# Range-check counts loaded ahead of the last chunk, its products in another order, and u's transposes in four PSUM buffers copied by two engines

## The chip, the cores and the metric

The kernel runs on one core of one Trainium2 chip. A core has a matrix engine (TensorE; PE in the profile, with its weight loads as PEld), a vector engine (VectorE, DVE), a scalar engine (ScalarE, ACT), GpSimd (POOL) and a queue engine that issues DMAs (SyncE, SP). Matmuls write to PSUM, a small memory in banks, and VectorE or ScalarE carry the results from there to SBUF, the working memory. Each engine works through its own list of instructions in the order in which they were written, and waits on semaphores for the others.

The metric is the device time of one execution in microseconds (us). The profile's span, from the first to the last instruction, is some 2 us shorter than that time.

## The reference

Two blocks follow each other. The first is attention with routing: for each of 4 batches and 8 heads, 768 queries and keys of 64 numbers are assigned to one of 16 centroids, and a query sees only the keys of its own centroid. The second is an MLP mixer over the 768 tokens of 512 channels:

```
scores = where(q_assign == k_assign, q @ k.T / 8, -1e9)
x      = softmax(scores) @ v            # heads side by side: (4, 768, 512)
h      = relu(x.T @ w_tok1) @ w_tok2    # over tokens, 768 -> 256 -> 768
u      = x + h.T
out    = u + relu(u @ w_ch1) @ w_ch2    # over channels, 512 -> 1536 -> 512
```

All of it is float32. The change lies in the last line of this, the channel products, and in what follows them.

## The kernel before

The work runs in three stages. Up to about 326 us, 16 pairs of heads go through the attention. Up to about 414 us come the token products: `tok1` and `tok2` of all four batches, which leave u in `xs[b]`, a tile of 128 partitions x 6 row blocks x 512 channels for each batch. The rest is the channel products of the four batches.

**The channel products.** Each is a product of 2 x 2 blocks, done with seven block products where the plain way has eight (a scheme of Strassen's kind): `left_weights`, `right_weights` and `turn_u` prepare sums and differences of the blocks, and `chunk` runs the seven products of one piece. A batch has two parts, and each part has three chunks of the first product (`ch1_chunk`, w_ch1 and the relu, results `h2`) and three chunks of the second (`ch2_chunk`, w_ch2, results added to `xs[b]` and, in part 1, sent to the output). A block product of `ch2_chunk` is three matmuls over 128 x 128 x 256, each of which the trace shows as two, so "x6" is one product.

**A chunk.** The products go to three PSUM tiles, tags X, Y and Z, of which pool `ps_m` has two buffers each. The order is written out by hand: p1 in X, then the left-over product c21 of the chunk before (list `late`, in that chunk's X), p5 in Z, c11 in Y, u2 in X, c12 in Z, c22 in X. Every product is followed by its `done`, which reads the PSUM tile: in `ch2_chunk` always a VectorE add, for p1, p5 and u2 into a kept tile, for the others into u. X is used again and again: u2, c22 and c21 go on adding to what p1 left in it, each after the result before it has been read. Z takes c12 on top of p5 in the same way. In part 1, c12 completes one block of 128 rows of the output and c21 another, and SyncE then issues its DMA (L707). After the very last chunk, `late.pop()()` runs its c21, so that c22 and c21 stand side by side there.

**turn_u.** Before the channel products of a batch, u must be transposed: `turn_u(b, n)` makes, for one half n of the rows, four PSUM tiles `pt` (f = 0 to 3) of three TensorE transposes each, and copies each to `uT`. With n = 1 it ends with four subtractions on VectorE, which make the sums `uTs` and change `uT`. It is called eight times: twice for batch 0 among the last `tok2` products, and for each later batch after the first and the second `ch2_chunk` of part 1 of the batch before. All four tiles have the tag Y, and ScalarE copies all four. The `tok2` products around the first two calls use the tags X and Z in turn (`mtile`).

**The range check.** The fast way is right only if certain sums lie in a range. `fits` and `fits_count` count the good partitions, early (about 529 us). `fits_load` reads the three counts into registers of every engine, and at L1077 every engine branches over a slow general version (`general`) if all are good, as they are here. `fits_load` stands behind everything else, after the last chunk. On SyncE each load comes with a check of its bounds.

Of the kernel before, what the change touches and what calls it, by code (L numbers as in the profile page):

```python
# [8 lines left out]
F32 = mybir.dt.float32  # L9
# [7 lines left out]
B, H, S, D = 4, 8, 768, 64  # L17
C = 16
P = 128
NJ = S // P  # L20
DM = H * D
# [5 lines left out]
HJ = NJ // 2  # L27
# [20 lines left out]
def kernel(  # L48
# [29 lines left out]
    nc = tc.nc  # L78
# [30 lines left out]
    pools = {}  # L109
# [424 lines left out]
    def sub(dst, a, b):  # L534
        nc.vector.tensor_tensor(out=dst, in0=a, in1=b, op=ALU.subtract)

    def add(dst, a, b):
        nc.vector.tensor_tensor(out=dst, in0=a, in1=b, op=ALU.add)  # L538
# [36 lines left out]
    def turn_u(b, n):  # L575

        if n == 0:
            pools["uT"] = pools["u"].tile([P, 2, NF, HS], F32, name="uT")
            pools["uTs"] = pools["u"].tile([P, 3, NF // 2, HS], F32, name="uTs")
        uT, uTs = pools["uT"], pools["uTs"]  # L580
        for f in range(NF):
            pt = pools["ps_m"].tile([P, HJ, P], F32, tag="Y", name="pt")
            for i in range(HJ):
                nc.tensor.transpose(  # L584
                    out=pt[:, i], in_=xs[b][:, HJ * n + i, f * P : (f + 1) * P], identity=ident
                )
            nc.scalar.copy(out=uT[:, n, f], in_=pt.rearrange("p i t -> p (i t)"))
        if n == 1:
            R = {"B11": uT[:, 0, 0:2], "B21": uT[:, 0, 2:4], "B22": uT[:, 1, 2:4]}
            R["T1"], R["T2"], R["T4"] = (uTs[:, i] for i in range(3))  # L590
            R["T3"] = b12 = uT[:, 1, 0:2]
            sub(R["T1"], b12, R["B11"])
            sub(R["T2"], R["B22"], R["T1"])
            sub(R["T3"], R["B22"], b12)
            sub(R["T4"], R["B21"], R["T2"])
            pools["R"] = R

    late = []

    def chunk(n, product, done):  # L600


        def ptile(tag):
            return pools["ps_m"].tile([P, n], F32, tag=tag, name="p" + tag)

        X = ptile("X")
        product(X, "A11", "B11", True)
        if late:
            late.pop()()
        done("p1", X)  # L610
        Z = ptile("Z")
        product(Z, "S1", "T1", True)
        done("p5", Z)
        Y = ptile("Y")
        product(Y, "A12", "B21", True)
        done("c11", Y)
        product(X, "S2", "T2", False)
        done("u2", X)
        product(Z, "S4", "B22", False)
        done("c12", Z)  # L620
        product(X, "S3", "T3", False)
        done("c22", X)

        def end():
            product(X, "A22", "T4", False)
            done("c21", X)

        late.append(end)

    def ch1_chunk(part, i):  # L630
# [17 lines left out]
        def done(name, psum):  # L648
# [24 lines left out]
            else:  # L673
                a = h2["A12"][:, i]
                nc.scalar.activation(out=a, in_=psum, func=ACT.Relu)
                sub(h2["S4"][:, i], a, h2["S2"][:, i])

        chunk(HS, product, done)

    def ch2_chunk(b, part, i):  # L680

        h2, Bw = pools["h2"], pools["B"]
        u = {
            f"c{r + 1}{c + 1}": xs[b][:, HJ * r + i, 256 * c : 256 * c + 256]
            for r in range(2)
            for c in range(2)
        }
        kept = {}
        takes = {"p1": "c11", "p5": "c22", "u2": "c12"}
        gives = {"c11": "p1", "c22": "p5", "c12": "u2"}  # L690

        def product(psum, a, w, start):
            for k in range(3):
                nc.tensor.matmul(  # L694
                    psum, lhsT=h2[a][:, k, i * P : (i + 1) * P], rhs=Bw[w][:, 3 * part + k],
                    start=start and k == 0, stop=k == 2, skip_group_check=not start,
                )

        def done(name, psum):
            if name in takes:  # L700
                kept[name] = pools["mlp"].tile([P, DM // 2], F32, name=name, bufs=2)
                add(kept[name], psum, u[takes[name]])
            else:
                add(u[name], psum, kept[gives[name]] if name in gives else u[name])
                if part == 1 and name in ("c12", "c21"):
                    j = i + HJ * (name == "c21")
                    nc.sync.dma_start(  # L707
                        out[b].rearrange("(p j) m -> p j m", p=P)[:, j], xs[b][:, j]
                    )

        chunk(DM // 2, product, done)

    good = const.tile([P, 3], F32, name="good")
    count = const.tile([1, 3], I32, name="count")
# [22 lines left out]
    def fits_load():  # L737

        loaded = [
            nc.values_load(count[0:1, i : i + 1], min_val=0, max_val=P) for i in range(3)  # L740
        ]
        return loaded[0] + loaded[1] + loaded[2]
# [127 lines left out]
    while ends:  # L870
        for _ in range(-(-len(beside) // len(ends))):
            beside.pop(0)()
        ends.pop(0)()
        if len(ends) in (11, 9):
            turn_u(0, len(ends) == 9)
# [4 lines left out]
    for b in range(B):  # L880
        for part in range(2):
            for i in range(3):
                ch1_chunk(part, i)
                for _ in range(2):
                    if beside:
                        beside.pop(0)()
            for i in range(3):
                ch2_chunk(b, part, i)
                if part == 1 and i < 2 and b + 1 < B:
                    turn_u(b + 1, i)  # L890
            if b == 0:
                (fits_count if part else fits)()
    late.pop()()
    both = fits_load()


    def general():
# [209 lines left out]
```

## Time and profile before

| What | Measured |
|---|---|
| time, median of 3 runs | 873.44 us (873.29 to 873.79) |
| span of the profiled execution | 871.6 us |
| granted TensorE clock, mean | 0.997 |
| transposes of turn_u (L584) | 96, median 273 ns a record, first at 394.2, last at 744.1 |
| copies of turn_u (L587) | 32 on ScalarE, median 479 ns |
| one VectorE copy of the same shape (L776) | 558 ns |
| matmul of a ch2 product (L694) | 379 ns a record |
| VectorE add of a ch2 product (L538) | 0.42 us |
| output DMAs (L707) | 24 of 256 KB, median 2.0 us from issue to landing |
| last matmuls start | 862.50 us |
| last add starts | 864.10 us |

How to read it: records of matmuls overlap, since the engine starts the next before the last one's modelled end; the pace of a row is the distance between starts, not the length of a record. In a timeline the columns are the start, the length from the first record's start to the last one's end, the engine, the line, the operation with output and inputs, the count, and in brackets how long the engine was idle before and who released it. In the view of one line of code the columns are engine, operation, count, the shortest, median and longest duration in ns, and the first and last start. A "q" behind an engine's name marks its own queue of control instructions (register loads, branches, semaphore events), which do not count as busy.

### The profile page before, as it was taken

How to read it: one execution, taken by the hardware profiler on the slowest of the kernel's cores; microseconds unless marked ns; L12 is line 12 of the kernel's file. 1: busy time of each engine (PE TensorE's matmuls, PEld its weight loads, DVE VectorE, ACT ScalarE, POOL GpSimd, SP SyncE). 2: the span in 40 equal slices, each digit the busy share in tenths (PEclk: the TensorE clock that was granted, in tenths of full speed). 3: DMA queues.
4: the chain of work that ended last, by engine and by line, in shares of the span. 5: the costliest groups of instructions: out<-in, count | busy, mean ns of one | idle time of the engine just before them, and what ended most of it. 6: DMA issues, size and time to landing. Idle time of an engine off the chain costs nothing.

```text
span 871.6 us, 11036 instructions
## 1 busy us (share of the span) xinstructions
PE 858.7 (99%) x4294; PEld 525.3 (60%) x4294; DVE 502.8 (58%) x848; ACT 296.6 (34%) x506; POOL 45.7 (5%) x40
## 2 busy tenths in 40 slices
PE   9999999999999999999999999999999999999996
PEld 4444444445444444444577686785876867768675
DVE  6878887989888852894553443424344333443332
ACT  5566566666656541421210312103112021130210
POOL 1001010101101000320000000000000000000000
PEclk9999999999999999999999999999999999999998
DMA  7855455576563300510000010000010000100001
GB/s 147 150 122 111 91 119 112 121 104 139 125 116 94 86 25 1 168 49 1 0 1 1 0 37 37 0 1 1 36 37 1 0 1 25 49 1 1 0 26 51
DMA packets 133275, 47.61 MB, mean 55 GB/s; under 512 B 122080, under 2 KB 126176, under 8 KB 133216
## 3 DMA queue, kind: packets, MB, share of 16 engines
q1 hardware_dynamic: 131616, 46.45, 24.0%
q8 instruction: 35, 0.57, 0.3%
q10 hardware_dynamic: 1600, 0.39, 0.2%
q14 instruction: 24, 0.20, 0.1%
HBM read 34.64 MB, written 6.29 MB: 47 GB/s over the span
## 4 chain that ended last, share of the span: by engine, by line
PE 94%; DVE 4%; ACT 1%; issue 0%; DVEq 0%
PE sc L420 18%; PE pX L694 14%; PE pX L643 14%; PE av L443 14%; PE pZ L694 7%; PE pZ L643 7%; PE ph L512 4%; PE pY L694 4%; PE pY L643 4%; PE pu L521 3%; PE px L472 1%; PE small L459 1%; PE pt L584 1%; PE small L301 1%; DVE wh L214 1%; DVE wT L219 1%
## 5 line engine op out<-in xcount | busy, mean ns | idle before, releaser
L425 ACT ACTIVATE ex<-sc 128x768 f32<-128x768 f32 x192 | 151.4, 812 | 71.1 <-PE av L443 36.5
L420 PE MATMUL sc<-qkT 64*128 64x384 f32 x768 | 155.0, 482 | 0.0
L433 DVE TENSOR_TENSOR sum<-sum,ex 128x768 f32<-128x768 f32 x128 | 127.7, 997 | 28.3 <-ACT ex L425 15.6
L443 PE MATMUL av<-ex,va 128*64 128x384 f32 x768 | 127.4, 488 | 0.0
L443 PEld LDWEIGHTS av<-ex,va 128*64 128x64 f32 x768 | 53.7, 137 | 71.7 <-issue 69.9
L420 PEld LDWEIGHTS sc<-qkT 64*128 64x128 f32 x768 | 67.9, 187 | 39.4 <-issue 39.4
L643 PE MATMUL pX<-uT,wc 128*128 128x384 f32 x192 | 67.4, 487 | 0.0
L420 PE MATMUL sc<-ohT 64*128 64x384 bf16 x384 | 62.7, 323 | 0.2 <-DVE ohT L393 0.2
L651 ACT COPY p<-pX 128x384 f32<-128x384 f32 x24 | 11.4, 475 | 148.1 <-PE pX L643 148.1
L643 PEld LDWEIGHTS pX<-uT,wc 128*128 128x128 f32 x192 | 36.2, 190 | 24.7 <-issue 1.0
L226 POOL TENSOR_TENSOR wc<-wT,wup 128x512 int32<-128x512 int32 x24 | 33.1, 1378 | 199.9 <-DVE wT L219 199.9
L512 PE MATMUL ph<-x,wt 128*128 128x512 f32 x96 | 42.1, 594 | 0.7 <-DVE x L524 0.7
L521 PE MATMUL pu<-h,wt 128*128 128x512 f32 x96 | 42.0, 592 | 0.0
L538 DVE TENSOR_TENSOR c<-pZ,u 128x384 f32<-128x384 f32 x24 | 13.4, 558 | 46.8 <-PE pZ L643 46.8
L420 PEld LDWEIGHTS <-ohT 64*128 64x128 bf16 x384 | 18.7, 94 | 33.2 <-issue 9.4
L538 DVE TENSOR_TENSOR x<-pX,x 128x256 f32<-128x256 f32 x24 | 10.2, 424 | 49.3 <-PE pX L694 49.3
L538 DVE TENSOR_TENSOR hA<-pY,p 128x384 f32<-128x384 f32 x24 | 13.4, 557 | 40.4 <-PE pY L643 40.4
L694 PE MATMUL pX<-w2s,hA 128*128 128x256 f32 x144 | 35.1, 380 | 0.5 <-DVE x L538 0.5
L694 PE MATMUL pX<-wc,hA 128*128 128x256 f32 x144 | 35.0, 379 | 0.0
L694 PE MATMUL pZ<-w2s,hS 128*128 128x256 f32 x144 | 35.0, 379 | 0.0
L694 PE MATMUL pY<-wc,hA 128*128 128x256 f32 x144 | 35.0, 379 | 0.0
L694 PE MATMUL pX<-w2s,hS 128*128 128x256 f32 x144 | 35.0, 379 | 0.0
(126 smaller groups left out, 1173.3 us busy)
## 6 DMA issues: line engine op xcount, KB each, us to landing
raw<-in_moe_w_ch_dram SPq DMA_DIRECT2D x24, 512.0 KB, 4.1
va<-in_v_dram SPq DMA_DIRECT2D x16, 384.0 KB, 3.2
out_dram<-x SPq DMA_DIRECT2D x24, 256.0 KB, 2.0
qk<-in_k_dram SPq DMA_DIRECT2D x60, 96.0 KB, 3.8
qk<-in_q_dram SPq DMA_DIRECT2D x60, 96.0 KB, 3.6
raw<-in_moe_w_tok_dram SPq DMA_DIRECT2D x3, 512.0 KB, 4.5
raw<-in_moe_w_tok_dram SPq DMA_DIRECT2D x4, 384.0 KB, 4.0
ex<-in_q_dram ACTq DMA_DIRECT2D x4, 96.0 KB, 3.3
```

The costliest lines, as they stand in the source:

```text
L214: nc.vector.tensor_scalar(out=h, in0=h, scalar1=0x07FFFFFF, scalar2=3, op0=ALU.bitwise_and, op1=ALU.logical_shift_left,)
L226: nc.gpsimd.tensor_tensor(out=dst.bitcast(I32), in0=T, in1=up, op=ALU.add)
L420: nc.tensor.matmul(sc[:, h, 0:HS], lhsT=src[rows, 1, j], rhs=src[rows, 0, js], start=start, stop=not start,)
L425: nc.scalar.activation(out=ex, in_=sc[:, :, 0:HS], func=ACT.Exp, scale=SM_SCALE)
L433: nc.vector.tensor_tensor(out=acc, in0=acc if j > 1 else st["ex", qh, 0], in1=st["ex", qh, j], op=ALU.add)
L443: nc.tensor.matmul(av[h * D : (h + 1) * D], lhsT=st["va"][:, h, j], rhs=ex[:, h], start=(j == 0), stop=(j == NJ - 1),)
L512: nc.tensor.matmul(pf, lhsT=W["tok1"][:, j, t * P : (t + 1) * P], rhs=xs[b][:, j], start=(j == 0), stop=(j == NJ - 1),)
L521: nc.tensor.matmul(pu, lhsT=W["tok2"][:, t, j], rhs=h1s[b][:, t], start=(t == 0), stop=(t == NT - 1))
L538: nc.vector.tensor_tensor(out=dst, in0=a, in1=b, op=ALU.add)
L643: nc.tensor.matmul(psum, lhsT=A[a][:, k, c * P : (c + 1) * P], rhs=R[r][:, k], start=start and k == 0, stop=k == 1, skip_group_check=not s ...
L651: nc.scalar.copy(out=kept[name], in_=psum)
L694: nc.tensor.matmul(psum, lhsT=h2[a][:, k, i * P : (i + 1) * P], rhs=Bw[w][:, 3 * part + k], start=start and k == 0, stop=k == 2, skip_grou ...
```

## The change

Three edits, in two groups.

The first group is in `turn_u`: the tiles pt take the tags Y and Z in turn, so that with two buffers each all four of a call have one of their own; and the copies of f = 1 and f = 3 go to VectorE. It is for letting the transposes of a call run without waiting for their copies.

The second group is at the end. `chunk` gets a flag for the very last chunk, which changes the order of its products from p1, (c21 before), p5, c11, u2, c12, c22, c21 to p1, (c21 before), p5, u2, c11, c22, c12, c21. It is for putting a product of another tile between the two that use X. And `fits_load` moves from behind everything to ahead of that last chunk, so that the engines have the counts in their registers by the end.

```diff
@@ turn_u
-            pt = pools["ps_m"].tile([P, HJ, P], F32, tag="Y", name="pt")
+            pt = pools["ps_m"].tile([P, HJ, P], F32, tag="YZ"[f % 2], name="pt")
...
-            nc.scalar.copy(out=uT[:, n, f], in_=pt.rearrange("p i t -> p (i t)"))
+            copy = nc.vector.tensor_copy if f % 2 else nc.scalar.copy
+            copy(out=uT[:, n, f], in_=pt.rearrange("p i t -> p (i t)"))
@@ chunk
-    def chunk(n, product, done):
+    def chunk(n, product, done, last=False):
...
-        product(Y, "A12", "B21", True)
-        done("c11", Y)
+
+        def product_y():
+            product(Y, "A12", "B21", True)
+            done("c11", Y)
+
+        def product_z():
+            product(Z, "S4", "B22", False)
+            done("c12", Z)
+
+
+        between = [product_y, product_z]
+        if not last:
+            between.pop(0)()
         product(X, "S2", "T2", False)
         done("u2", X)
-        product(Z, "S4", "B22", False)
-        done("c12", Z)
+        between.pop(0)()
         product(X, "S3", "T3", False)
         done("c22", X)
+        if last:
+            between.pop(0)()
@@ ch2_chunk
-        chunk(DM // 2, product, done)
+        chunk(DM // 2, product, done, b == B - 1 and part == 1 and i == 2)
@@ the loop over the batches
             for i in range(3):
+                if b == B - 1 and part == 1 and i == 2:
+                    both = fits_load()
                 ch2_chunk(b, part, i)
...
     late.pop()()
-    both = fits_load()
```

## The prediction

> **What bounds the kernel now.** I read the page first: the share of each engine, then the tenths in 40 slices, then the chain that ended last.
>
> ```profile
> span 871.6 us, 11036 instructions
> ...
> PE 858.7 (99%) x4294; PEld 525.3 (60%) x4294; DVE 502.8 (58%) x848; ACT 296.6 (34%) x506; POOL 45.7 (5%) x40
> ...
> PE 94%; DVE 4%; ACT 1%; issue 0%; DVEq 0%
> ```
>
> TensorE (PE) is busy 99% of the span and is 94% of the chain, at a granted clock of 0.997. VectorE (DVE) stands at 58%, ScalarE (ACT) at 34%, and in the second half, where the change lies, at 3 to 4 and 0 to 2 tenths a slice. So time comes only from three places: holes in the stream of matmuls, extra matmuls (the change has none), and what runs after the last matmul. The list of waits has the holes that concern the change:
>
> ```profile
> PEld pt L584 <- ACT uT L587: 3.8, 8, 0.5
> ...
> PE pt L584 <- ACT uT L587: 1.9, 8, 0.2
> ...
> PE pX L694 <- DVE x L538: 0.5, 1, 0.5
> ```
>
> Columns: total us, times, longest. Eight times, once in each call of turn_u, the transposes wait for ScalarE's copies; once, at the end, a product waits for a VectorE add. Then the timeline of one turn (of the eight, all alike):
>
> ```profile
> 517.59 0.82 PE L584 MATMUL pt<-ident,x 128*128 128x128 f32 x6
> 517.79 0.42 DVE L538 TENSOR_TENSOR x<-pX,p 128x256 f32<-128x256 f32 x1 [0.87 <-PE pX L694]
> 518.12 0.86 ACT L587 COPY uT<-pt 128x384 f32<-128x384 f32 x2 [8.91 <-PE pt L584]
> ...
> 518.65 0.93 PE L584 MATMUL pt<-ident,x 128*128 128x128 f32 x6 [0.24 <-ACT uT L587]
> ...
> 519.41 0.38 PE L694 MATMUL pX<-wc,hA 128*128 128x256 f32 x1
> ```
>
> Six transposes start within 0.82 us; the last one's record is 0.273 us long (the median of that row), so they start (0.82 - 0.273)/5 = 0.109 us apart. Twelve would take 1.31 us. The turn takes 519.41 - 517.59 = 1.82. **The hole is 0.51 us a turn**, more than the 0.24 that the wait shows, since a matmul's modelled end lies behind the start of the next. Last, the tail: the timeline's last add, and the engines' own queues at the lines of the register loads (L740) and of the branch (L1077).
>
> ```profile
> 864.10 0.42 DVE L538 TENSOR_TENSOR x<-pX,x 128x256 f32<-128x256 f32 x1 [1.65 <-PE pX L694]
> ```
> ```profile
> L740 PEldq TENSOR_LOAD <-count x3: 306/306/495, 862.5 to 863.5; - x3
> ...
> L740 SPq TENSOR_LOAD <-count x3: 262/280/519, 864.9 to 866.4; - x3
> ```
> ```profile
> L1077 PEldq COMPARE_BRANCH  x1: 3336/3336/3336, 864.0 to 864.0; - x1
> ...
> L1077 SPq COMPARE_BRANCH  x1: 58/58/58, 867.1 to 867.1; - x1
> ```
>
> The last add ends at 864.52, SyncE (SP) issues the last output until 864.88, and only then loads its three counts, one after the other, each with its bounds check; it reaches the branch at 867.1, its next semaphore event at 869.6, and the span ends at 871.6. SP is the last engine there: PE's next event is at 867.4, DVE's at 868.6.
>
> [...] from branch to next event it is 2.5 us on SP, 2.7 on ACT, 2.9 on DVE, 3.4 on PE, and 0.2 on POOL. This stays in the changed kernel. [...] a DVE copy of 128x384 from 6.80 for 0.56 us overlaps an ACT copy from 7.12 for 0.48, each at its usual length.
>
> **Part A, the transposes.** Each turn makes four tiles of three transposes. Two buffers (tag Y) become four (Y, Z, Y, Z), and the second and fourth copies move to VectorE, so no tile of a turn waits for a copy of the same turn. Gain at most 8 x 0.51 = 4.1 us.
> What takes some of it back:
> - Are the Z buffers free? In the six turns among the channel products, the last Z product is c12, whose add ends about 0.7 us before the turn (in the chunk before it, 516.49 + 0.42 = 516.9 against 517.59): nothing. In the first two turns the last tok2 tile is a Z tile and its add runs beside the transposes (394.80 + 0.69 = 395.49); the fourth tile's weight load would come at 394.60 + 8 x 0.109 = 395.47, and a release takes some 0.05: 0.07 us each, 0.14 in all.
> - A VectorE copy of this shape costs 0.56 us (one row, L776, 558 ns; ACT 479), 32 copies becoming 16 and 16. Behind it in the turns with n = 0 nothing waits for over 3 us (DVE's next add is at 511.31 in the turn at 506.70): nothing. With n = 1 the four subtractions of uTs (0.875 us apart) are queued behind it. Now they start at 519.01. Then: fourth tile ready at 517.59 + 11 x 0.109 + 0.273 = 519.06, copy from 519.10, first subtraction at about 519.57 (a 384-element pass passes the engine in 0.47), the second after the first has ended, 520.65, the fourth at 522.4, then the adds for c21 at 523.27 and p1 at 523.6, which ends at 524.02. The product u2 waits for this p1 add, because it goes on adding to X. It would start at 518.90 + 4 x 1.296 = 524.08, its weights 0.2 earlier, so it is 0.1 us late, 0.2 at most; in three turns 0.3 (0 to 0.6). Before, p1's add had ended at 523.49 against 524.60.
>
> A gains 4.1 - 0.14 - 0.3 = **3.65** (3.3 to 4.1).
>
> **Part B, order of the last chunk.** Now c22 and c21 stand side by side in X, so c21 waits until c22's result is added: its matmul starts at 862.50, where 860.53 + 1.296 = 861.82 was due, and its own pace is disturbed by a further 0.10 (the record is 1.56 us instead of 1.46). With c12, in Z, between them, c22's add (0.42 + 0.2) lies beside c12's 1.296. Gain 0.68 + 0.10 = 0.78. The other neighbours, p5 then u2: u2 needs p1's add, which ends at 856.30, against its start at 856.64: nothing. The row of output that c12 completes goes out 1.3 us later, still 1.3 us ahead of the last one: nothing.
>
> **Part B, the counts.** On SP, 864.88 to 867.1 shrinks to the branch's own arithmetic, some 0.15 us: 2.05 gained. The loads' new place costs SP nothing (idle from 852.5 to 856.0; they need 2.1). DVE passes them behind c22's add at 852.96, done by 854.5, and its next add is due at 855.55. ACT and POOL have none of the chunk's work. On PE they stand behind the c22 product of the chunk before, which is released when u2's add ends, about 850.84; from there c12 and c22 give work until 852.75, and the loads take 1.3 us (862.51 to 863.83 now), ending at 852.2, with the next product's weight load due at 852.54: nothing, if the queue holds those 18 instructions and a load needs no idle engine. It needs none at 862.51, where it starts with 1.2 us of that product still to be issued.
> Against this, SP's fetch now begins at 864.3, while the last output is on its way. Undisturbed it took 2.5; DVE's, at that place, 2.9; PE's 3.4. I take 2.9: 0.4 lost (0 to 0.9).
>
> B gains 0.78 + 2.05 - 0.4 = **2.4** (1.9 to 2.8). PE and DVE, without their loads, pass their branches earlier too and stay ahead of SP.
>
> **Sum**: 873.44 - 3.65 - 2.4 = **867.4**.
>
> **Rivals.**
> 1. VectorE becomes a bound in the turns with n = 1: the copies push the subtractions further than I think and u2 takes back all of 0.51 in three turns, and the fourth tiles wait longer in the first two. A is then 8 x 0.51 - 3 x 0.51 - 0.3 = 2.3: 868.7. For: a margin of nearly zero. Against: my chain already charges the second subtraction a full wait on the first.
> 2. PE's loads drain it: from the end of c22, 852.9, 1.3 us of loads and a cold start, 1.5 lost: 868.9. Against: the start at 862.51.
> 3. The tail is set by something not seen in it (the landing of the last output, or fetches that hinder each other), and B gives its 0.78 alone: 869.0.
> 4. Slower: copies of two engines hinder each other and the transposes, so that each turn loses 0.4 instead of gaining (+3.2), PE's loads drain it (+1.5), and B gains 2.4: +2.3, 875.7. Nothing but the unknown speaks for it.
>
> **Chances.** My sum 0.73 (866.5 to 868.1), rival 1 0.09, rival 2 0.10, rival 3 0.04, rival 4 0.02, a mild failure of both parts that ends near no change 0.02. The range runs from 866.4, all bounds good, to 868.9, which takes in the first two rivals. Faster by 0.2% (below 871.7): 0.96; within 0.02; slower 0.02.
>
> **What the profile after would show.** Turns of 1.31 us from first transpose to next matmul, about 1.38 in the first two; no wait of PE for uT; COPY rows of L587 on ACT x16 and DVE x16. p1's add after the turns with n = 1 ending within 0.2 us of u2's start. No wait of PE for x in the last chunk; its matmuls 1.296 apart to the end. PE's loads at about 850.8 less A's gain, with no hole at the next product; SP's branch within 0.3 us of its last issue. I am wrong if a hole of over 1 us follows PE's loads, if turns stay over 1.5 us, or if SP's wait behind the branch grows past 3.4 us.

## The result, and the profile after

The changed kernel takes **867.35 us** (median of 6 runs, 866.91 to 867.70) against 873.43 (873.29 to 873.79): a ratio of 0.993 with a 95% interval of 0.9917 to 0.9943, 6.1 us or 0.7% faster. A second set of runs gave 866.95 against 873.45, 6.5 us.

First the page of the changed kernel, its head and its chain. The counts of engine instructions show what was moved: 16 copies from ACT (506 to 490) to DVE (848 to 864).

```profile
span 864.8 us, 11041 instructions
...
PE 856.0 (99%) x4294; PEld 525.0 (61%) x4294; DVE 511.0 (59%) x864; ACT 290.7 (34%) x490; POOL 45.8 (5%) x40
...
PE 94%; DVE 4%; issue 0%; DMA 0%; DVEq 0%; ACT 0%
```

PE's work is the same 4294 matmuls, in a span 6.8 us shorter. Next the timeline of the turn that the prediction showed, in the changed kernel, and on to the product u2.

```profile
515.83 1.47 PE L584 MATMUL pt<-ident,x 128*128 128x128 f32 x12
...
516.36 0.48 ACT L588 COPY uT<-pt 128x384 f32<-128x384 f32 x1 [9.24 <-PE pt L584]
516.69 1.21 DVE L588 COPY uT<-pt 128x384 f32<-128x384 f32 x2 [0.23 <-PE pt L584]
517.01 0.48 ACT L588 COPY uT<-pt 128x384 f32<-128x384 f32 x1 [0.17 <-PE pt L584]
...
517.14 1.46 PE L707 MATMUL pX<-wc,hA 128*128 128x256 f32 x6
517.82 0.95 DVE L535 TENSOR_TENSOR uTs<-uT 128x768 f32<-128x768 f32 x1
...
521.82 0.41 DVE L538 TENSOR_TENSOR p<-pX,x 128x256 f32<-128x256 f32 x1
...
522.29 0.73 PEld L707 LDWEIGHTS pX<-w2s,hS 128*128 128x128 f32 x4 [0.20 <-DVE p L538]
```

All twelve transposes now stand in one row without a wait, and the turn takes 517.14 - 515.83 = 1.31 us. The price is in the lower half: VectorE's copies end at 517.90, the first subtraction starts 1.99 us after the turn (1.42 before), p1's add ends at 522.23, and the weight load of u2, due at about 522.11, comes at 522.29. It stands 0.2 us ahead of its matmul, so of these 0.18 us only 0.07 reach the row of matmuls. Then the tail: the last products in the timeline, and the engines' own queues at the line of the loads (now L753) and of the branch (L1091).

```profile
855.10 1.46 PE L707 MATMUL pX<-wc,hS 128*128 128x256 f32 x6
...
856.39 1.46 PE L707 MATMUL pZ<-wc,hS 128*128 128x256 f32 x6
...
857.69 1.46 PE L707 MATMUL pX<-w2s,hA 128*128 128x256 f32 x6
...
858.34 1.63 SPq L720 DMA_DIRECT2D out_dram<-x  x2
859.19 0.42 DVE L538 TENSOR_TENSOR x<-pX,x 128x256 f32<-128x256 f32 x1 [0.87 <-PE pX L707]
```
```profile
L753 PEldq TENSOR_LOAD <-count x3: 305/306/495, 846.7 to 847.7; - x3
L753 SPq TENSOR_LOAD <-count x3: 267/278/514, 848.4 to 849.8; - x3
```
```profile
L1091 SPq EVENT_SEMAPHORE  x8: 17/17/17, 862.9 to 863.5; - x8
...
L1091 SPq COMPARE_BRANCH  x1: 57/57/57, 860.1 to 860.1; - x1
```

c22, c12 and c21 start 1.29 to 1.30 us apart, up to the end. The loads on PE run from 846.73 to 848.04, and the timeline around them goes on at its pace (848.62 - 847.33 = 1.29):

```profile
847.33 1.46 PE L707 MATMUL pX<-wc,hS 128*128 128x256 f32 x6
...
848.41 1.27 PEld L707 LDWEIGHTS pX<-wc,hA 128*128 128x128 f32 x6
848.62 1.46 PE L707 MATMUL pX<-wc,hA 128*128 128x256 f32 x6
```

SP's last issue ends at 859.97 and its branch stands at 860.1, where 2.2 us lay between them before. Its next event comes 2.8 us behind the branch, where it was 2.5. The prediction and the expectations call such a wait a fetch; that it is one was the author's inference and is not shown.

### The profile page after: what moved, and what is told of

Same layout as the page of the kernel before. It is cut to its first block, busy times and chain, and to the rows that moved or that the text cites. A ratio compares the mean times of both kernels' runs of the same rounds, so it can differ in the third digit from the quotient of the medians.

```text
span 864.8 us, 11041 instructions
## 1 busy us (share of the span) xinstructions
PE 856.0 (99%) x4294; PEld 525.0 (61%) x4294; DVE 511.0 (59%) x864; ACT 290.7 (34%) x490; POOL 45.8 (5%) x40
## 4 chain that ended last, share of the span: by engine, by line
PE 94%; DVE 4%; issue 0%; DMA 0%; DVEq 0%; ACT 0%
PE sc L420 18%; PE pX L707 14%; PE pX L656 14%; PE av L443 14%; PE pZ L707 7%; PE pZ L656 7%; PE ph L512 4%; PE pY L707 4%; PE pY L656 4%; PE pu L521 3%; PE px L472 1%; PE small L459 1%; PE pt L584 1%; PE small L301 1%; DVE wh L214 1%; DVE wT L219 1%
```

## The experiments

All are edits of the changed kernel or, for one part alone, of it with the other parts put back. Each time stands against that of the kernel before, measured beside it. "PE's last matmul" below is the end of its record in the trace, less the difference with which the two traces start (see the repeat).

**The changed kernel again**, as a yardstick.

> The changed kernel itself, once more, as the yardstick for the runs beside it. Theory (holes closed, loads hidden): 867.35 us as before, turns of 1.31 us, three holes of 0.07 us before u2 after the turns with n = 1, no hole at TensorE's register loads. The first measurements spread over 866.9 to 867.7 where the kernel before spreads over 873.3 to 873.8; if the spread is in the fetch behind SyncE's branch, this profile shows there another length than 2.73 us; if it is in the loads at the start, another offset of the first matmuls.

Measured: 866.95 us (866.88 to 867.79). The turns, the three small holes and SP's wait behind the branch (from the branch's start to the next event, 2.79 us in both profiles of this kernel; 2.73 from its end) are the same to 0.01 us. What differs is the start: one early group of transposes, in the timelines of this run and of the first one.

```profile
12.41 0.51 PE L385 MATMUL po<-identb,oh 128*128 128x128 bf16 x6
```
```profile
12.12 0.51 PE L385 MATMUL po<-identb,oh 128*128 128x128 bf16 x6
```

In the kernel before it stands at 12.40. So some 0.3 us of the spread between runs is decided in the first 12 us, which the change does not touch; what decides it there stays open.

**Part A alone.**

```diff
-                if b == B - 1 and part == 1 and i == 2:
-                    both = fits_load()
...
-        chunk(DM // 2, product, done, b == B - 1 and part == 1 and i == 2)
+        chunk(DM // 2, product, done)
...
     late.pop()()
+    both = fits_load()
```

> Part A alone: four buffers and two engines in turn_u; order and loads at the end as before. Theory: eight holes of 0.51 us go, three of 0.07 come: 873.43 - 3.9 = 869.5. Rival (the gain is mostly in the tail): above 871.

Measured: 869.86 us against 873.66, ratio 0.9954 (0.9941 to 0.9968): 3.8 us. PE's last matmul ends 3.86 us sooner than in the kernel before, and the hole of 0.68 before it is back.

**The order alone** (turn_u and the loads as before).

> Of part B only the order of the products in the last chunk; turn_u and loads as before. Theory: the hole of 0.68 us before the last product and the 0.10 in it go, everything behind them moves by 0.78: 872.65; SyncE's fetch stays at 2.5 us. Rival (the end is set by the output DMAs or another engine): 873.4.

Measured: 872.97 us against 873.66, ratio 0.9992 (0.9985 to 0.9999): 0.7 us. The timeline of PE in this run has the last four products at an even pace:

```profile
858.39 1.46 PE L707 MATMUL pY<-wc,hA 128*128 128x256 f32 x6
859.69 1.46 PE L707 MATMUL pX<-wc,hS 128*128 128x256 f32 x6
860.98 1.46 PE L707 MATMUL pZ<-wc,hS 128*128 128x256 f32 x6
862.28 1.46 PE L707 MATMUL pX<-w2s,hA 128*128 128x256 f32 x6
```

Behind the branch SP waits 2.6 us, as before within 0.1.

**The early loads alone** (turn_u and the order as before).

> Of part B only the register loads ahead of the last chunk; order and turn_u as before. Theory: SyncE goes from its last issue to the branch 2.05 us sooner, its fetch takes 2.75 us instead of 2.5 since the last output is then on its way: 873.43 - 1.8 = 871.6; no hole in the matmuls at TensorE's loads. Rival (TensorE's loads cost it a pause that other gains covered): 872.9.

Measured: 871.68 us against 873.66, ratio 0.9977 (0.9968 to 0.9987): 2.0 us. PE's matmuls run without a hole past its loads. The branch's line in this run:

```profile
L1091 SPq EVENT_SEMAPHORE  x8: 17/17/17, 868.2 to 868.7; - x8
...
L1091 SPq COMPARE_BRANCH  x1: 58/58/58, 865.4 to 865.4; - x1
```

2.8 us from branch to event, with the last issue ending at 865.26. In the runs where SP branches after its loads (before, part A alone, order alone) it is 2.53 to 2.61; in those where it branches right behind the last issue, 2.70 to 2.90. That the output in flight is what lengthens the wait fits both groups. So does another cause: SP's wait overlaps VectorE's by 1.5 to 2.0 us in the first group and by 2.1 to 2.4 in the second, so the two waits may hinder each other. Nothing here shows either or separates the two.

The three parts sum to 3.80 + 0.69 + 1.98 = 6.5 us, against 6.1 and 6.5 for the whole: they add up within the spread of the runs, and none shows that it needs another.

**Buffers or engine?** Three versions of turn_u take the two edits of part A apart. Four buffers, ScalarE alone:

```diff
-            copy = nc.vector.tensor_copy if f % 2 else nc.scalar.copy
+            copy = nc.scalar.copy
```

> Four buffers, but ScalarE makes all four copies, as before the change. Theory (the buffers are what closes the hole, the second engine is not needed and costs something): turns of 1.31 us, the first subtraction 1.42 us after the turn's start instead of 1.99, p1's add 0.6 us earlier, no hole before u2; 0.2 us less than the changed kernel, 867.15. Rival (ScalarE's four copies, 0.38 us apart, are too slow for transposes of 0.33 a tile): the turns stay over 1.5 us and 2 us or more are lost, 869.4.

Measured: 866.86 us (866.57 to 866.93) beside 866.95 of the changed kernel, whose runs reach up to 867.79: by the clock the two can't be told apart. By the trace PE's last matmul ends 0.21 us sooner than in the changed kernel, the three holes of 0.07. Repeated later on another occasion:

> The version with four buffers and four ScalarE copies once more, as the yardstick for the run with ScalarE's issue on the same chip: 866.9 us, no hole before u2, SyncE's branch within 0.2 us of its last issue.

Measured: 866.56 us (866.09 to 867.11), no hole before u2. In the timeline of the first of these runs the turn keeps its 1.31 us with ScalarE alone, and the subtractions start sooner:

```profile
515.84 1.47 PE L584 MATMUL pt<-ident,x 128*128 128x128 f32 x12
...
516.37 1.63 ACT L588 COPY uT<-pt 128x384 f32<-128x384 f32 x4 [8.75 <-PE pt L584]
...
517.15 1.46 PE L707 MATMUL pX<-wc,hA 128*128 128x256 f32 x6
517.26 0.96 DVE L535 TENSOR_TENSOR uTs<-uT 128x768 f32<-128x768 f32 x1 [0.80 <-ACT uT L588]
```

ScalarE's four copies, 0.38 us apart where a tile's transposes take 0.33, fall behind and last until 518.00, long after PE has left; with a buffer for each tile nothing on PE waits for them. Two engines, two buffers:

```diff
-            pt = pools["ps_m"].tile([P, HJ, P], F32, tag="YZ"[f % 2], name="pt")
+            pt = pools["ps_m"].tile([P, HJ, P], F32, tag="Y", name="pt")
```

> Two engines copy, but all tiles have tag Y, two buffers, as before the change. Theory (buffers): the third tile waits for the first one's ScalarE copy (ready 1.06 us after the start, as before), the fourth for the second one's VectorE copy (1.46 us), so the turn keeps its hole, 1.85 us, and VectorE's copies put off the subtractions further: 871.4. Rival (the second engine is what helps): turns of about 1.4 us, 868.

Measured: 871.28 us against 873.45, ratio 0.9975 (0.9965 to 0.9985): 2.2 us, which is part B less what the second engine costs here. The timeline has the wait back:

```profile
517.43 0.82 PE L584 MATMUL pt<-ident,x 128*128 128x128 f32 x6
...
518.49 0.96 PE L584 MATMUL pt<-ident,x 128*128 128x128 f32 x6 [0.24 <-ACT uT L588]
...
519.28 1.03 PE L707 MATMUL pX<-wc,hA 128*128 128x256 f32 x4
```

519.28 - 517.43 = 1.85 us a turn, 0.03 more than before the change, and u2 is again 0.07 late in three turns, 0.4 us in all. So **the buffers are the whole gain** of part A; the second engine gives nothing and costs 0.2 us with four buffers and 0.4 with two. Last, VectorE alone, with four buffers (`copy = nc.vector.tensor_copy`):

> Four buffers, VectorE makes all four copies. This pushes the suspected cost, the subtractions being queued behind copies on VectorE. Theory: turns still 1.31 us; copies at about 0.55, 1.02, 1.49 and 1.96 us from the turn's start, first subtraction at 2.43 instead of 1.99, so the hole before u2 grows from 0.07 to about 0.5 us in the three turns with n = 1, and only there: 868.7. Rival (VectorE's queue has slack that hides it): 867.4.

Measured: 868.11 us, 1.2 above the changed kernel. The turns stay at 1.31 us; the wait before u2 grows, in this version's list of waits (us in total, times, longest):

```profile
PEld pX L707 <- DVE p L538: 1.6, 3, 0.5
```

It costs PE 0.41 us each time, against 0.07 in the changed kernel, and PE's last matmul ends 1.05 later. The wait comes in the three turns with n = 1 and in no other: p1's add stands behind VectorE's copies and ends 1.54 us after c11's first matmul (521.07), where it is 1.20 in the changed kernel.

**How far are PE's loads hidden?** Two kernels load the counts twice at the same place.

```diff
-                    both = fits_load()
+                    spare = fits_load()
+                    both = fits_load()
```

> The changed kernel with the three counts loaded twice over at the same place (the first three values are not used). Theory (loads run in program order on TensorE and are hidden only while its queue holds work): six loads take about 2.5 us against 1.95 us of queued work less the weight load's lead, so a hole of about 0.9 us opens before the last chunk's first product: 868.3. Rival (loads run beside the queue without holding up what follows): no hole, 867.4.

Measured: 867.91 us, but not for the expected reason: the lists of PE, DVE, ACT and POOL contain three loads and three semaphore events in place of the unused ones, and PE's three end at 848.4, just in time. PE's part of the loads' line:

```profile
L753 PEldq EVENT_SEMAPHORE  x3: 51/51/51, 846.7 to 847.0; - x3
L753 PEldq TENSOR_LOAD <-count x3: 306/308/491, 847.1 to 848.1; - x3
```

On SyncE, where the six loads are there with their checks, the time goes at the very end: between two steps of its last drain lie 0.99 us (864.1 to 865.1), where it is 0.07 in the changed kernel. Its list is 9 instructions longer (334 against 325). What it waits for is not shown; one kind of DMA packet goes with such waits. In every run SP's next event behind the branch comes 1.1 to 1.4 us after an 8 KB packet of the instruction queue q14 has landed; here such a packet lands at 863.97, and the drain goes on 1.11 later (1.23 in the next kernel). In the changed kernel one lands at 863.97 too, but all of SP's steps are over by 864.80. Whose packets these are the trace doesn't say, so a wait for instructions is no more than the author's guess. In the next kernel all six values are used:

```diff
-                    both = fits_load()
+                    both = fits_load() + fits_load()
...
-    with tc.If(both < 3 * P):
+    with tc.If(both < 6 * P):
```

> The changed kernel with the three counts loaded twice and all six values used in the branch's sum (compared with 6 x 128), so that no engine can leave the loads out, as TensorE's list did in the run of the doubled loads. Theory (TensorE takes its loads in program order; they are hidden only as far as its queue holds work): six loads from 846.7 us, the first 0.6 and the others 0.41 apart, end at 849.3, where the next weight load is due at 848.4: a hole of 0.7 to 1.0 us before the last chunk's first product. Total 868.1 if nothing else comes; the longer list of SyncE may add the 1.0 us in its last drain that the run before showed, 869.1. Rival (loads run beside the queue): no hole, 867.2 (or 868.2 with the drain).

Measured: 869.14 us, against 873.86 of the kernel before. PE's part of the loads' line, and two stretches of the timeline of this run:

```profile
L753 PEldq TENSOR_LOAD <-count x6: 305/308/580, 847.4 to 849.6; - x6
```
```profile
847.97 1.46 PE L707 MATMUL pX<-wc,hS 128*128 128x256 f32 x6
```
```profile
849.05 0.38 PE L707 MATMUL pX<-wc,hS 128*128 128x256 f32 x1
849.47 0.42 DVE L538 TENSOR_TENSOR x<-pX,p 128x256 f32<-128x256 f32 x1 [0.87 <-PE pX L707]
850.20 1.16 PEld L707 LDWEIGHTS pX<-wc,hA 128*128 128x128 f32 x6 [1.18 <-issue]
850.24 1.53 PE L707 MATMUL pX<-wc,hA 128*128 128x256 f32 x6 [0.80 <-issue]
```

The loads start at 847.37, before the last product ahead of them (c22, at 847.97), and the last one ends at 850.18; the next weight load comes 0.02 later. From 849.05 the next matmul was due 0.22 later and comes at 850.24: a hole of 0.97 us, and the wait is marked "issue", since no semaphore explains it. So the loads on PE did hold up what stood behind them, and three of them cost nothing because the products ahead lasted longer (848.62 - 846.73 = 1.89 us to the next product's start, against loads of 1.31). By the two traces this kernel ends 2.2 us later than the changed one, less the difference at the start: PE's last matmul ends 1.04 later, and between the two steps of SyncE's drain lie 1.04 us again, 0.97 more.

**A version that goes on.** If SyncE is last by its branch, the wait behind it and its row of semaphore events, another engine should issue the last row of output. The kernel is the version with four buffers and ScalarE's copies, with this edit added:

```diff
-                    nc.sync.dma_start(
+                    last = b == B - 1 and i == 2 and name == "c21"
+                    (nc.scalar if last else nc.sync).dma_start(
```

> As the version with four ScalarE copies, and the very last output DMA is issued by ScalarE instead of SyncE. Theory (SyncE ends last, by its late branch, its fetch of 2.8 us and its 16 semaphore events in a row): SyncE branches 1.3 us earlier, after the row that c12 completes, and is through its events when ScalarE, whose branch now waits for the last issue and whose fetch takes 2.5 to 2.8 us, comes to its drain; the last drain of SyncE is then set by ScalarE's at about 862.9 us of the profile, 1.0 us sooner than before: 865.9. Rival (the landing of the last output or another engine sets the end): 866.9, no change.

Measured: **865.65 us** (865.51 to 866.39), beside 866.56 of that version with SyncE's issue; ratio to before 0.9909 (0.9894 to 0.9924). By the two traces, less the difference at the start, it ends 1.04 us sooner. It is the fastest kernel here. Its branch's line:

```profile
L1092 SPq EVENT_SEMAPHORE  x8: 17/17/17, 861.5 to 862.1; - x8
...
L1092 ACTq COMPARE_BRANCH  x1: 54/54/54, 859.9 to 859.9; - x1
...
L1092 ACTq EVENT_SEMAPHORE  x1: 17/17/17, 862.9 to 862.9; - x1
```

SP has come to the last of its row of events at 862.59 and stays there until 862.93: ACT comes back from its branch at 862.9, 2.9 us behind it. ACT is now the last, and the span is 863.8.

## Why the prediction was right

The predicted 867.4 met 867.35. Point by point, from the two profiles:

- **The turns, 4.1 us at most**: six of 1.310 and two of 1.33 for eight of 1.826, 4.08 us. Right; the buffer experiments show that the buffers alone do it.
- **The Z buffers of the first two turns, 0.07 us each**: 0.02 each. The fourth tile's weight load did come 0.07 late (395.28 where 395.21 was due), as worked out. But a weight load stands ahead of its matmul, and most of its lateness never reached the row of matmuls; the sum had charged all of it.
- **u2 after the turns with n = 1, 0.1 us, three times**: 0.067 three times, again less than the 0.18 of its weight load. The chain was right in its steps: first subtraction at +1.99 us (1.98 worked out), p1's add ending at +6.40 (6.43). The VectorE-only version, where this wait grows to 0.41, shows that it is this queue.
- **Part A**: 3.65 predicted; 3.88 by these holes, and in the run of A alone 3.86 by the trace and 3.8 by the clock.
- **The order, 0.78**: 0.68 + 0.10 are gone from PE; 0.76 by the trace and 0.69 by the clock in the run of the order alone.
- **SP's loads, 2.05**: the way from last issue to branch fell from 2.20 to 0.15 us. Right.
- **SP's wait behind the branch, 0.4 lost**: 0.26 (2.79 for 2.53). The 0.4 was an estimate from DVE's wait of 2.9 before the change; DVE waits longer than SP in every run here (2.9 to 3.3).
- **PE's loads, nothing**: no hole, and the six loads show that this was a matter of the margin of 0.37 us (loads over at 848.04, next weight load at 848.41). That the queue holds the 18 instructions was the author's assumption. The trace shows the first load start at 846.73 with eight matmuls and seven weight loads ahead of it in program order still to start.

Summed from the profiles, part B is 0.78 + 2.05 - 0.26 = 2.57 (2.4 predicted) and the whole 6.45, which is also the difference of the two spans (6.72) less that of the starts (0.28). The first median, 6.1, lies at my sum partly because its runs spread by 0.8 us; the second pass gave 6.5. So the true gain is probably some tenths above the forecast, and the agreement to 0.05 us is luck.

Rival 1, VectorE as a bound, was the right mechanism at a small part of its size (0.2 us where it had 1.5). Rival 2 fails at three loads. At six a hole of 0.97 opens, but not in its way: it let the loads begin only at the end of c22, and they begin before c22 does (847.37 against 847.97). Its cold start was an estimate; the product behind the hole took 1.37 us from start to start (850.24 to 851.61), 0.07 more than the 1.30 of the others. Of rival 3, waits that hinder each other may be in the 0.26 of SP's wait behind the branch; the 1.6 us that it took from part B show in no run. Nor does rival 4: copies of 479 to 482 ns on ACT and 557 to 559 on DVE are as long as before.

What the prediction left open: it charged A's copies on VectorE as a cost, but did not ask whether the second engine was needed at all. ScalarE's copies, 0.38 us apart in the trace before, are slower than the 0.33 of a tile's transposes, but with a buffer for each tile a burst of four need not wait for them.

## What to carry to other kernels

When a producer waits for a consumer within a short burst, count the buffers before adding a second consumer: here, with a buffer for each of its four tiles, the burst needed no faster consumer (1.31 us a turn with ScalarE alone or with both), and the helper's queue had other work behind it (u2 0.07 us late in three turns). In a stream of matmuls read the distance between starts, not the idle time, to see what a hole is worth (0.51 against 0.24 us here). At the end of a kernel follow each engine's own queue to the last instruction: here the loads and checks of the one that came last counted in full (2.05 us between last issue and branch), and it paid both to move them ahead (2.0 us alone) and to hand that engine's last task to an idle one (1.04 us).

## What the runs showed of the hardware

- The register loads that stand in PE's list between products ran while matmuls ahead of them had yet to start (847.37 against 847.97), and held up what stood behind them (last load over at 850.18, next weight load at 850.20). Three took 1.31 us, with 1.9 us from their start to the next product's, and cost nothing; six took 2.81 us and opened a hole of 0.97.
- The weight loads that came late cost PE less than their lateness: 0.18 us late cost 0.07, and 0.07 late cost 0.02.
- The taken branch at the end cost each engine its own time: 2.5 to 2.9 us on SP, 2.4 to 2.9 on ACT, 2.9 to 3.3 on DVE, 3.4 to 4.1 on PE, and 0.2 on POOL. On SP and ACT the next event came 1.0 to 1.4 us after an 8 KB packet of the instruction queue had landed, in every run.
- In both kernels with nine more instructions on SP, its last drain was 1 us longer (0.99 and 1.04 us between two steps that lie 0.07 apart in the changed kernel); why is not shown.
